# Second product of 24 leaves in seven half-width block products, with VectorE block sums

## The chip, the cores and the metric

The kernel runs on one core of one Trainium2 chip. The metric is the device time of one execution in microseconds (us). The engines have names in the profile: PE is the tensor engine (PEld its weight loads), DVE is VectorE, ACT is ScalarE, POOL is GpSimd, SP issues most transfers.

## The reference

`x` has 4 batches of 3072 tokens and 256 features. The reference takes the real part of a two-dimensional Fourier transform over tokens and features and then runs two feed-forward layers:

```
h = max(x @ w_in, 0);  u, v = h[..., :512], h[..., 512:]
v_n = (v - mean(v)) / sqrt(var(v) + 1e-6)
v_s = einsum('ts,bsd->btd', w_spatial, v_n) + b_spatial
x2 = (u * v_s) @ w_out                       # 512 features to 256
gate = 1 / (1 + exp(-(x2 @ w_gate)));  out = (gate * (x2 @ w_val)) @ w_out2
```

The change touches the product with `w_out`, called the second product here.

## The kernel before

**Number format.** Every matrix operand is split in a high and a low part (float32r). `mm3` (L259) makes three matmuls of one product: high x high, high x low, low x high (L261, L262, L263). The high part is a copy on ACT, the low part a subtraction on DVE.

**Stages.** First the transform and the product with `w_in` (to about 254 us). Then the product over tokens with `w_spatial` in "leaves" (to about 1751 us). Then the last feed-forward layer in 144 groups.

**Leaves.** The product over tokens is a seven-product scheme on 2x2 blocks: for each of two batch pairs `p`, seven products `i` in `ORDER` (L234), each in three column parts `c`: 42 leaves. A leaf has six steps `kp`, each of 24 matmuls of 512 columns into four PSUM banks `ps[d]`. The banks alternate between two sets of four. The stretch of the span in which PE works on one leaf is called a slot below; it lasts 32.64 us, or 38.08 us with a second product in it.

**Order of the work.** There is no scheduler: each engine runs its instructions in the order of the program text. At the beginning of each of the first four steps, `evacuate` (L1211) takes one bank `d` of the leaf before: DVE adds it to accumulators. For four of the seven products (`FINAL`, L236; 24 leaves) a token block of the gate is then complete: DVE multiplies by `u` (L1240), ACT copies the high part (L1246) and DVE forms the low part one step later (L1248). Then `advance` (L963) prepares operands `LEAD` = 3 steps ahead: loads on SP's queue, normalization on ACT (L916), sums or differences of blocks on DVE (L929, L933), high part on ACT (L942), low part on DVE (L950). In the last column part (`c` = 2) it also prepares the `v` operands of the next product. Loads go to seven tiles in rotation, and a load waits until the low part that last read its tile is done. `side_loads` (L1262) at the fifth step loads the bias and two `u` tiles, behind those loads on SP's queue. The matmuls of the step follow.

**The second product** of the leaf before runs after the fifth and after the sixth step of a slot (`second`, L1276): for each half `o` of the 256 outputs, four blocks `d` of 128 features, `mm3` each: 24 matmuls of 512 columns per leaf, into two banks that `evacuate` has emptied. ACT copies each bank to `x2` (L1287) and issues one store (L1289).

**The end of the stage.** The last slot (L1414 to 1467) orders its matmuls by bank, evacuates both the leaf before and its own banks 0 to 2, splits weights of the next stage and runs steps of the first operands there (`x_steps`, L1343). In the first feed-forward group (`n` = 0, L1552) come `p12` (two products, DVE adds them at L1484), the evacuation of bank 3, the split of "t1" (`steps[6]`), `p67`, both halves of the last second product (L1579, L1580) and `p5`, which uses "t1" (L1524).

Of the kernel before, what the change touches and what calls it, by code (L numbers as in the profile page):

```python
# [23 lines left out]
DM = 256  # L24
FF2 = 1536
P = 128
# [134 lines left out]
def layouts(x, moe_w_in, moe_w_spatial, moe_b_spatial, moe_w_out, moe2_w_gate, moe2_w_val, moe2_w_out):  # L161
# [18 lines left out]
    for at in (0, 32, 64):  # L180
# [6 lines left out]
    wg, wv = (w.reshape(2, P, 12, P) for w in (moe2_w_gate, moe2_w_val))  # L187
    arrays = {
# [6 lines left out]
        "w_out": moe_w_out.reshape(4, P, DM).transpose(1, 0, 2).reshape(P, 2, 512),  # L195
# [44 lines left out]
def tile_kernel(ctx: ExitStack, tc: tile.TileContext, t: dict, out: bass.AP):  # L240
# [927 lines left out]
    wo = [gp.tile([P, 2, 512], F32R, tag=f"wo{n}", name=f"wo{n}") for n in "hl"]  # L1168
# [3 lines left out]
    taken, begun, stores = [], [], []  # L1172

    def background():
# [5 lines left out]
        elif begun:  # L1180
            first, kind, i = begun.pop()
            value, = from64_rest(first, new())
            if kind == "second":
                split(wo[0][:, i, :], wo[1][:, i, :], value)
            elif kind == "out":
                stores.append((wv_d[i // 2][:, i % 2 * 512 : i % 2 * 512 + 512], value))
            else:
# [11 lines left out]
                stores.append((wg_d[i][:, 0:384], value[:, 0:384]))  # L1199
                stores.append((wg_d[i][:, 384:896], sums))  # L1200
        else:
            for to, value in stores:
                nc.sync.dma_start(to, value)
            stores.clear()
# [6 lines left out]
    def evacuate(leaf, ps, d, side):  # L1211
# [6 lines left out]
        if i in FINAL:  # L1218
            g = gp.tile([P, 512], F32, tag="cv", name="g", bufs=4)
# [21 lines left out]
        if "parts" in side:  # L1241
            gh, gl = (x[at] for x in side["parts"])
        else:
            gh = gp.tile([P, 512], F32R, tag="gh", name="gh", bufs=4)
            gl = gp.tile([P, 512], F32R, tag="gl", name="gl", bufs=4)
        nc.scalar.copy(gh, g)  # L1246
        finish_gate(side)
        side["low"] = lambda: nc.vector.tensor_tensor(out=gl, in0=g, in1=f(gh), op=ALU.subtract)  # L1248
        side["g"].append((gh, gl))
        if d < 2:  # L1250
            load_u(side, d + 2)

    def finish_gate(side):
        if "low" in side:
            side.pop("low")()
# [20 lines left out]
    def second(leaf, o, bank, side):  # L1276

        p, i, c = leaf
        mem, th = FINAL[i]
        finish_gate(side)  # L1280
        ps = banks(bank)
        for d in range(4):
            at = (d % 2) * 256 + o * P
            mm3(ps, [w[:, d // 2, at : at + P] for w in wo], side["g"][d], d == 0, d == 3)
        if o == 0:
            side["x2"] = gp.tile([P, 2, 512], F32, tag="x2", name="x2", bufs=1)
        nc.scalar.copy(side["x2"][:, o, :], ps)  # L1287
        if o == 1:
            nc.scalar.dma_start(x2_d[(2 * p + mem) * 6 + 3 * th + c], side["x2"])  # L1289
# [68 lines left out]
    def load_raw(j):  # L1358
        raw = []
        for c, n in zip(pairs[j], "hl"):  # L1360
            r = gp.tile([P, 2, 512], F32, tag=f"wo{n}", name="raw")
            nc.sync.dma_start(r, x2_d[c])
            raw += [r[:, 0, :], r[:, 1, :]]
        return raw
# [14 lines left out]
    for n, leaf in enumerate(leaves[:-1]):  # L1379
# [3 lines left out]
        side = {"g": []}  # L1383
        for kp in range(6):
            if before is not None:
                if kp < 4:
                    evacuate(before[0], before[1][kp], kp, before[2])
                else:
                    finish_gate(before[2])
# [15 lines left out]
            if before is not None:  # L1405
                if kp >= 4 and before[0][1] in FINAL:
                    second(before[0], kp - 4, 4 - base + kp - 2, before[2])
# [9 lines left out]
    side = {"g": []}  # L1417
# [19 lines left out]
    finish_gate(before[2])  # L1437
# [3 lines left out]
    side["parts"] = [cp.tile([P, 4, 512], F32R, tag=f"c0{k}", name=f"tail{k}") for k in range(2)]  # L1441
# [190 lines left out]
```

## Time and profile before

| | |
|---|---|
| median of 3 runs | 2842.18 us (2842.17 to 2842.79) |
| the profiled execution | 2841.18 us |
| its span, first to last instruction | 2839.1 us |
| PE busy | 2827.8 us, 12630 matmuls |
| DVE busy | 1998.9 us |
| ACT busy | 1416.4 us |
| granted PE clock | 1.0 (2.4 GHz) over the span |

The span leaves out about 2 us around the instructions. A matmul's row is longer than its distance to the next one, since matmuls are pipelined; the distances of starts tell the pace.

### The profile page before, as it was taken

Reading aid. Unit: us, or ns where it says so; the run is one execution under the profiler, and the core shown is the slowest. Engines: PE = TensorE matmul, PEld = TensorE weight load, DVE = VectorE, ACT = ScalarE, POOL = GpSimd, SP = SyncE. Lnnn points to the kernel's source line nnn. Section 1 sums busy time; section 2 is a strip of 40 time slices with the busy share of each in tenths; the row PEclk is TensorE's granted clock in tenths of the full one; section 3 lists DMA queues with packets and bytes.
Section 4 is the critical chain, followed back from the end, with each engine's and each line's share of the span. In section 5 each row is a group of like instructions: output and inputs, shape, how many; then the busy total and the mean of one; then the engine's idle time right before and its main releaser. Section 6 shows DMA issues by size and latency. Waiting matters only on the chain.

```text
span 2839.1 us, 34286 instructions
## 1 busy us (share of the span) xinstructions
PE 2827.8 (100%) x12630; PEld 2360.2 (83%) x12630; DVE 1998.9 (70%) x2936; ACT 1416.4 (50%) x2264; POOL 235.5 (8%) x348
## 2 busy tenths in 40 slices
PE   9999999999999999999999999999999999999999
PEld 7998888888888888888888888888888888888887
DVE  8877757778847666677756666876667666766665
ACT  6886434334424424433424424665655565656565
POOL 5984000011000000000000000000000000000000
PEclk9999999999999999999999999999999999999999
DMA  8888757778847766677866683100000000000000
GB/s 300 292 314 324 274 198 260 266 261 299 275 143 261 257 227 238 213 268 262 284 207 213 214 285 108 61 23 30 30 30 1 30 30 30 23 8 30 30 15 15
DMA packets 150953, 470.89 MB, mean 166 GB/s; under 512 B 16769, under 2 KB 18689, under 8 KB 150401
## 3 DMA queue, kind: packets, MB, share of 16 engines
q1 hardware_dynamic: 144448, 440.52, 45.0%
q0 software_dynamic: 2448, 14.82, 1.4%
q10 hardware_dynamic: 3888, 13.37, 1.2%
q8 instruction: 98, 1.61, 0.2%
q14 instruction: 71, 0.57, 0.1%
HBM read 386.07 MB, written 82.58 MB: 165 GB/s over the span
## 4 chain that ended last, share of the span: by engine, by line
PE 96%; DVE 2%; DMA 1%; ACT 1%; issue 0%; SPq 0%; ACTq 0%; DVEq 0%
PE bank L261 30%; PE bank L262 30%; PE bank L263 30%; PE psv L262 1%; PE psv L263 1%; PE psv L261 1%; PE psu L261 1%; PE psu L262 1%; PE psu L263 1%; PE psf L261 1%; PE psf L262 1%; PE psf L263 1%; DMA st<-v_d 1%; PE psv L730 0%; PE psu L768 0%
## 5 line engine op out<-in xcount | busy, mean ns | idle before, releaser
L262 PE MATMUL bank<-wl,vh 128*128 128x512 f32 x2016 | 784.4, 389 | 0.2 <-DVE wl L950 0.2
L261 PE MATMUL bank<-wh,vh 128*128 128x512 f32 x2016 | 784.3, 389 | 0.0
L263 PE MATMUL bank<-wh,vl 128*128 128x512 f32 x2016 | 784.2, 389 | 0.0
L942 ACT CAST wh<-st 128x1024 fp32r<-128x1024 f32 x249 | 260.9, 1049 | 382.9 <-PE bank L263 231.0
L262 PEld LDWEIGHTS bank<-wl,vh 128*128 128x128 f32 x2016 | 378.4, 188 | 79.5 <-DVE wl L950 0.8
L261 PEld LDWEIGHTS bank<-wh,vh 128*128 128x128 f32 x2016 | 378.4, 188 | 78.5
L263 PEld LDWEIGHTS bank<-wh,vl 128*128 128x128 f32 x2016 | 378.4, 188 | 78.3
L950 DVE TENSOR_TENSOR wl<-st,wh 128x1024 fp32r<-128x1024 f32 x249 | 306.8, 1233 | 169.4 <-ACT wh L942 168.9
L261 PE MATMUL bank<-x,wgh 128*128 128x512 f32 x673 | 262.4, 390 | 0.5 <-ACT t L1511 0.4
L1497 DVE TENSOR_TENSOR t<-t,bank 128x512 f32<-128x512 f32 x144 | 98.9, 687 | 231.4 <-PE bank L263 231.4
L262 PE MATMUL bank<-x,wgh 128*128 128x512 f32 x673 | 261.8, 389 | 0.0
L263 PE MATMUL bank<-x,wgl 128*128 128x512 f32 x673 | 261.8, 389 | 0.0
L933 DVE TENSOR_TENSOR st<-st 128x1024 f32<-128x1024 f32 x177 | 217.7, 1230 | 50.5 <-DMA st<-in_wt 50.5
L1520 DVE TENSOR_TENSOR gl<-s,gh 128x512 fp32r<-128x512 f32 x288 | 199.4, 692 | 57.8 <-ACT gh L1518 44.4
L262 PE MATMUL bank<-gl,wv 128*128 128x512 f32 x576 | 224.1, 389 | 0.0
L261 PE MATMUL bank<-gh,wv 128*128 128x512 f32 x576 | 224.1, 389 | 0.0
L263 PE MATMUL bank<-gh,wv 128*128 128x512 f32 x576 | 224.1, 389 | 0.0
L916 ACT ACTIVATE st<-st,ln_all 128x512 f32<-128x512 f32 x162 | 123.3, 809 | 140.5 <-DMA st<-v_d 115.7
L1485 ACT ACTIVATE s<-s 128x512 f32<-128x512 f32 x144 | 91.0, 632 | 153.8 <-DVE s L1484 153.7
L261 PEld LDWEIGHTS bank<-x,wgh 128*128 128x128 f32 x673 | 126.3, 188 | 28.5 <-ACT s L1482 0.9
L263 PEld LDWEIGHTS bank<-x,wgl 128*128 128x128 f32 x673 | 126.3, 188 | 26.3
L262 PEld LDWEIGHTS bank<-x,wgh 128*128 128x128 f32 x673 | 126.3, 188 | 26.0
(267 smaller groups left out, 4490.4 us busy)
## 6 DMA issues: line engine op xcount, KB each, us to landing
st<-in_wt SPq DMA_DIRECT2D x424, 512.0 KB, 5.5
st<-v_d SPq DMA_DIRECT2D x140, 512.0 KB, 4.7
u_d<-tu SPq DMA_DIRECT2D x64, 384.0 KB, 5.4
u<-u_d SPq DMA_DIRECT2D x96, 256.0 KB, 5.7
v_d<-tv SPq DMA_DIRECT2D x92, 256.0 KB, 5.1
x_d<-x ACTq DMA_DIRECT2D x24, 512.0 KB, 4.9
raw<-x_d SPq DMA_DIRECT2D x24, 512.0 KB, 7.1
xt<-in_xh SPq DMA_DIRECT2D x23, 512.0 KB, 5.2
```

The source lines that it names most:

```text
L261: nc.tensor.matmul(out=ps, lhsT=w[0], rhs=x[0], start=first, stop=False, **kw)
L262: nc.tensor.matmul(out=ps, lhsT=w[0], rhs=x[1], start=False, stop=False, **kw)
L263: nc.tensor.matmul(out=ps, lhsT=w[1], rhs=x[0], start=False, stop=last, **kw)
L916: nc.scalar.activation(st[:, k, :], st[:, k, :], AF.Identity, scale=scale[:, at], bias=shift[:, at])
L933: nc.vector.tensor_tensor(out=tiles[0], in0=tiles[0], in1=tiles[1], op=op)
L942: nc.scalar.copy(hl[0], st)
L950: eng.tensor_tensor(out=hl[1], in0=st, in1=f(hl[0]), op=ALU.subtract)
L1485: nc.scalar.activation(s1, s1, AF.Sigmoid)
L1497: nc.vector.tensor_tensor(out=g["t2"], in0=g["t2"], in1=g["b"], op=ALU.add)
L1520: nc.vector.tensor_tensor(out=l, in0=s, in1=f(h), op=ALU.subtract)
```

## The change

The second product is computed by the same kind of seven-product scheme. The 512 features of a leaf are two pairs of blocks of 128, the 512 tokens two halves of 256. Per pair there are seven terms, each `mm3` on 256 columns: 42 matmuls of 256 columns per leaf. The weights' sums and differences are formed once in the background work (POOL and DVE). Per pair DVE makes four differences of 128x256, and the operands of the terms are four pieces (one of 256 columns, three of 512), each with a high and a low part. Each piece has one buffer for both pairs. Four banks accumulate the seven terms over both pairs.

Six terms of the first pair run after the third step of a slot, the seventh after the fourth, all seven of the second pair after the fifth. `combine` then makes the outputs from the four banks: one copy on ACT and six additions on DVE; it stands in front of the sixth step's preparations. Two stores of half the size replace one. In the last leaf, six terms run before the feed-forward stage, the seventh in its first group and the second pair in its second group; the raw operands of the second pair of chunks are loaded one group later. All four banks of the other set are used instead of two.

```diff
@@ def background():
-            if kind == "second":
-                split(wo[0][:, i, :], wo[1][:, i, :], value)
...
+                for at, src in ((slice(0, 384), value[:, 0:384]), (slice(384, 896), sums)):
+                    if kind == "second":
+                        split(wo[0][:, i, at], wo[1][:, i, at], src)
@@ def evacuate(leaf, ps, d, side):
         nc.vector.scalar_tensor_tensor(out=g, in0=side["u"][d], scalar=0.0, in1=g, op0=ALU.max, op1=ALU.mult)
-        nc.scalar.copy(gh, g)
-        finish_gate(side)
-        side["low"] = lambda: nc.vector.tensor_tensor(out=gl, in0=g, in1=f(gh), op=ALU.subtract)
-        side["g"].append((gh, gl))
         if d < 2:
             load_u(side, d + 2)
+        finish_gate(side)
+        if d % 2 == 0:
+            side["raw"] = g
+            if d == 0:
+                take_piece(side, 0, 0, g[:, 0:HC])
+            return
+        b1, b2 = side.pop("raw"), g
+        if d == 1:
+            take_piece(side, 0, 1, b2)
+        else:
+            take_piece(side, 1, 0, b1[:, 0:HC])
+            side["late"] = lambda: take_piece(side, 1, 1, b2)
...
+        for to, x, y in (
+            (ta[:, 0:HC], b1[:, HC:], b1[:, 0:HC]),
+            (tb[:, 0:HC], b2[:, HC:], b1[:, HC:]),
+            (ta[:, HC:], b2[:, HC:], ta[:, 0:HC]),
+            (tb[:, HC:], b2[:, 0:HC], ta[:, HC:]),
+        ):
+            tt(out=to, in0=x, in1=y, op=ALU.subtract)
+        take_piece(side, d // 2, 2, ta)
+        take_piece(side, d // 2, 3, tb)
+    HC = 256
+    def take_piece(side, pair, i, src):
...
+        nc.scalar.copy(hi, src)
+        side["g"][pair, i] = (hi, lo)
+        side["lows"].append(lambda: nc.vector.tensor_tensor(out=lo, in0=src, in1=f(hi), op=ALU.subtract))
+    TERMS = {
+        1: ("a11", 0, 0, 0, 0), 6: ("s2", 2, 1, 0, 1), 5: ("s1", 2, 0, 1, 0), 7: ("s3", 3, 0, 1, 1),
+        3: ("s4", 1, 1, 2, 0), 4: ("a22", 3, 1, 2, 1), 2: ("a12", 1, 0, 3, 0),
+    }
+    def combine(side, part, both, to):
+        x, y, z, w = (side["acc"][k] for k in range(4))
+        nc.scalar.copy(p1, x[:, 0:HC])
+        tt(out=u2, in0=p1, in1=x[:, HC:], op=ALU.add)
+        tt(out=both, in0=u2 (twice), in1=y, op=ALU.add)
+        tt(out=to[1][:, HC:], in0=both[:, HC:], in1=y[:, 0:HC], op=ALU.add)
+        tt(out=to[0][:, HC:], in0=both[:, 0:HC], in1=z[:, 0:HC], op=ALU.add)
+        tt(out=to[1][:, 0:HC], in0=both[:, HC:], in1=z[:, HC:], op=ALU.add)
+        tt(out=to[0][:, 0:HC], in0=p1, in1=w[:, 0:HC], op=ALU.add)
@@ the loop over leaves
+            if final and kp == 4:
+                before[2].pop("late")()
+                finish_gate(before[2])
+            if final and kp == 5:
+                combine_cv(before[2])
             advance(6 * n + kp + LEAD, 2)
...
-            if before is not None:
-                if kp >= 4 and before[0][1] in FINAL:
-                    second(before[0], kp - 4, 4 - base + kp - 2, before[2])
+            if final and kp in (2, 3, 4):
+                second(before[2], kp // 4, ((1, 6, 5, 7, 4, 3), (2,), (1, 6, 5, 7, 4, 3, 2))[kp - 2], 4 - base)
+            if final and kp == 5:
+                send(before[0], before[2])
@@ the last slot
         if d == 0:
+            second(before[2], 0, (1, 6, 5, 7, 4, 3, 2), 4 - base)
+            before[2].pop("late")()
+            finish_gate(before[2])
...
         if d == 1:
-            second(before[0], 0, 4 - base + 2, before[2])
+            second(before[2], 1, (1, 6, 5, 7, 4, 3, 2), 4 - base)
+            combine_cv(before[2])
...
         if d == 2:
-            second(before[0], 1, 4 - base + 3, before[2])
+            send(before[0], before[2])
...
+    second(side, 0, (1, 6, 5, 7, 4, 3), base)
@@ the feed-forward groups
         if n == 0:
             evacuate(leaf, ps[3], 3, side)
+            second(side, 0, (2,), base)
+            side.pop("late")()
             finish_gate(side)
             steps[6]()
...
+            if n == 1:
+                second(side, 1, (1, 6, 5, 7, 4, 3, 2), base)
...
-            second(leaf, 0, base, side)
-            second(leaf, 1, base + 1, side)
+        if n == 1:
+            combine(side, x[:, 2, :], x[:, 3, :], [last_x2[:, o, :] for o in range(2)])
+            send(leaf, side)
...
-            if fb == 0:
+            if fb == (j == 0):
                 next_steps = x_steps(j + 1, load_raw(j + 1))
```

## Rows read from the trace of the kernel before

**Rows 1.** The page, part 1: busy time, share and instructions of each engine.

```profile
PE 2827.8 (100%) x12630; PEld 2360.2 (83%) x12630; DVE 1998.9 (70%) x2936; ACT 1416.4 (50%) x2264; POOL 235.5 (8%) x348
```

**Rows 2.** Timeline of PE, a leaf: start, length, line, shape; 36 rows between.

```profile
1299.77 0.39 PE L263 MATMUL bank<-wh,vl 128*128 128x512 f32 x1
...
1308.15 0.39 PE L261 MATMUL bank<-wh,vh 128*128 128x512 f32 x1
```

**Rows 3.** Timeline of weight loads and matmuls at a restart of PE.

```profile
1331.88 0.19 PEld L262 LDWEIGHTS bank<-wl,vh 128*128 128x128 f32 x1 [0.64 <-DVE wl L950]
1331.99 0.19 PEld L263 LDWEIGHTS bank<-wh,vl 128*128 128x128 f32 x1
...
1331.88 0.50 PE L262 MATMUL bank<-wl,vh 128*128 128x512 f32 x1 [0.22 <-DVE wl L950]
1332.21 0.40 PE L263 MATMUL bank<-wh,vl 128*128 128x512 f32 x1
```

**Rows 4.** Windows, one slot each: length, then busy time and instructions of each engine.

```profile
422.80:460.88 38.08, 38.08 (x170) 31.53 (x169) 31.63 (x38) 22.79 (x28) 0.00 (x0) 1.00 0.82 275
460.88:498.95 38.07, 38.07 (x169) 31.53 (x168) 27.45 (x33) 9.89 (x12) 0.00 (x0) 1.00 0.68 235
...
732.88:770.96 38.08, 38.08 (x170) 31.53 (x169) 32.13 (x39) 22.62 (x28) 0.00 (x0) 1.00 0.89 287
...
1712.64:1750.72 38.08, 38.08 (x169) 31.54 (x168) 25.17 (x34) 15.22 (x23) 0.00 (x0) 1.00 0.31 100
```

The columns after the length are PE, PEld, DVE, ACT, POOL, the granted PE clock, the DMA share and GB/s.

**Rows 5.** Timeline of PE in the transform, 384 columns; 8 rows between.

```profile
116.47 0.33 PE L261 MATMUL psf<-c,fh 128*128 128x384 f32 x1
...
118.03 0.33 PE L446 MATMUL psf<-spc,sps 128*128 128x384 f32 x1
```

**Rows 6.** Groups by line and shape: weight loads of the second product; busy, mean ns.

```profile
L261 PEld LDWEIGHTS bank<-gh,woh 128*128 128x128 f32 x184 | 34.5, 188 | 7.2
```

**Rows 7.** Timeline of DVE: 512 columns in the slot from 422.80, then 256 columns.

```profile
427.34 0.68 DVE L1224 TENSOR_TENSOR c<-bias,bank 128x512 f32<-128x512 f32 x1
427.94 0.68 DVE L1240 SCALAR_TENSOR_TENSOR g<-u,g 128x512 f32<-128x512 f32 x1
...
1760.97 0.42 DVE L257 TENSOR_TENSOR wgl<-wst,wgh 128x256 fp32r<-128x256 f32 x1
```

**Rows 8.** Timeline of DVE: third gate multiplications, and a fourth block's low part.

```profile
471.51 0.68 DVE L1240 SCALAR_TENSOR_TENSOR g<-u,g 128x512 f32<-128x512 f32 x1
...
747.30 0.68 DVE L1240 SCALAR_TENSOR_TENSOR g<-u,g 128x512 f32<-128x512 f32 x1
...
760.78 0.69 DVE L1248 TENSOR_TENSOR gl<-g,gh 128x512 fp32r<-128x512 f32 x1
```

**Rows 9.** Timeline of DVE from 422.80: its idle times, with what ended them.

```profile
425.60 1.23 DVE L950 TENSOR_TENSOR wl<-st,wh 128x1024 fp32r<-128x1024 f32 x1 [3.01 <-ACT wh L942]
...
456.99 1.46 DVE L929 SCALAR_TENSOR_TENSOR st<-st,ln_all 128x512 f32<-128x512 f32 x2 [2.36 <-ACT st L916]
...
461.86 0.69 DVE L1224 TENSOR_TENSOR c<-bias,bank 128x512 f32<-128x512 f32 x1 [1.40 <-DMA bias<-in_bt]
```

**Rows 10.** Timeline of ACT: the copy of the second product's bank.

```profile
423.00 0.59 ACT L1287 COPY x<-bank 128x512 f32<-128x512 f32 x1 [5.21 <-PE bank L263]
```

**Rows 11.** Timeline of DVE and PE in the first feed-forward group.

```profile
1752.36 0.68 DVE L1484 TENSOR_TENSOR s<-s,bank 128x512 f32<-128x512 f32 x1
...
1755.66 0.69 DVE L257 TENSOR_TENSOR x<-raw,x 128x512 fp32r<-128x512 f32 x1
...
1759.35 0.39 PE L261 MATMUL bank<-x,wgh 128*128 128x512 f32 x1
```

More of the change, by code (lines that the diff above doesn't have):

```diff
@@ L1172, in tile_kernel, with send_stores @@
     taken, begun, stores = [], [], []
+    def send_stores():
+        for to, value in stores:
+            nc.sync.dma_start(to, value)
+        stores.clear()
     def background():
@@ L1182, in background @@
             value, = from64_rest(first, new())
-            if kind == "second":
-                split(wo[0][:, i, :], wo[1][:, i, :], value)
-            elif kind == "out":
+            if kind == "out":
                 stores.append((wv_d[i // 2][:, i % 2 * 512 : i % 2 * 512 + 512], value))
@@ L1274, in side_loads, with second @@
                 load_u(side, d)
-    def second(leaf, o, bank, side):
+    TERMS = {
+        1: ("a11", 0, 0, 0, 0),
+        6: ("s2", 2, 1, 0, 1),
+        5: ("s1", 2, 0, 1, 0),
+        7: ("s3", 3, 0, 1, 1),
+        3: ("s4", 1, 1, 2, 0),
+        4: ("a22", 3, 1, 2, 1),
+        2: ("a12", 1, 0, 3, 0),
+    }
+    def second(side, pair, terms, bank):
+        for term in terms:
+            w, piece, half, acc, at = TERMS[term]
+            first = acc not in side["acc"]
+            if first:
+                side["acc"][acc] = banks(bank + acc)
+            w = slice(W_AT[w] * P, W_AT[w] * P + P)
+            mm3(
+                side["acc"][acc][:, at * HC : at * HC + HC],
+                [x[:, pair, w] for x in wo],
+                [x[:, half * HC : half * HC + HC] for x in side["g"][pair, piece]],
+                first,
+                pair == 1,
+                skip_group_check=True,
+            )
@@ L1278, in second, with combine_cv, send @@
+    def combine_cv(side):
+        combine(side, *(lambda a: (a[0], a[1], a[2:]))([gp.tile([P, 512], F32, tag="cv", name="y", bufs=4) for _ in range(4)]))
+    def send(leaf, side):
         p, i, c = leaf
         mem, th = FINAL[i]
[L1280 to L1286, printed above, removed]
@@ L1287, in second @@
-        nc.scalar.copy(side["x2"][:, o, :], ps)
-        if o == 1:
-            nc.scalar.dma_start(x2_d[(2 * p + mem) * 6 + 3 * th + c], side["x2"])
+        for o in range(2):
+            nc.scalar.dma_start(x2_d[(2 * p + mem) * 6 + 3 * th + c][:, o, :], side["to"][o])
     p, i, c = leaves[-1]
@@ L1436, in tile_kernel @@
         evacuate(before[0], before[1][d], d, before[2])
-    finish_gate(before[2])
     wv0 = [cp.tile([P, 8, DM], F32R, tag=f"c1{k}", name=f"wv{k}") for k in range(2)]
     wvs += [[x[:, 0:4, :] for x in wv0], [x[:, 4:8, :] for x in wv0]]
-    side["parts"] = [cp.tile([P, 4, 512], F32R, tag=f"c0{k}", name=f"tail{k}") for k in range(2)]
+    side["spare"] = cp.tile([P, 4, 512], F32, tag="c00", name="spare")
     steps = x_steps(0, [raw[:, k, :] for k in range(4)])
@@ L1558, in tile_kernel @@
         if n == 0:
+            side["parts"] = [cp.tile([P, 4, 512], F32R, tag=f"c0{k}", name=f"tail{k}") for k in range(2)]
             evacuate(leaf, ps[3], 3, side)
+            second(side, 0, (2,), base)
+            side.pop("late")()
             finish_gate(side)
```

76 lines of the change are left out of this document (48 added, 28 removed).

## The prediction

> **What bounds the kernel now.** I read the page's engine totals first: the tensor engine (PE) is busy for the whole span, VectorE for 70% and ScalarE for 50% [rows 1]. A busy PE can still be a PE that waits inside its rows, so the next view is the order of the matmuls: 37 steps between the two rows of 128x512 take 8.38 us, 0.2265 us each, and nothing but PE itself lies between them [rows 2]. In the two stages after the transform (leaves, then feed-forward) the stream is gapless, apart from a handful of waits of 0.1 to 0.6 us; the restart in [rows 3] is one of the largest. So time is saved only by a shorter stream, and lost by every new wait of PE. The last view is VectorE per slot (the stretch in which PE works on one leaf): it differs widely around its mean. In the slot from 422.80 it is busy for 31.63 of 38.08 us, in the next for 27.45, in the one from 732.88 for 32.13 [rows 4]. That is where a VectorE that gets more work can become the bound.
>
> **What the change does to PE.** Per leaf the second product goes from 24 matmuls of 512 columns to 42 of 256 (7 terms, 2 pairs, 3 parts each). The sizes in the trace are 512 columns at 0.2265 us [rows 2] and 384 at 1.56 us for 9 steps, 0.1733 us [rows 5]. The line through both falls by 0.0532 per 128 columns and gives 0.120 for 256. So 5.44 us become 42 x 0.120 = 5.04: 0.40 less per leaf, 9.6 for the 24 leaves. No row has this kind of matmul at 256 columns. Bounds: in proportion (0.113) it is 16.1 less; with no gain below 384 columns (0.173) it is 44 more. I take the line, because the thing that could break it, the load of weights ahead of each matmul, is shown at a restart to be fast enough: the second load starts 0.11 us after the first, and the restarting matmul starts its successor 0.33 us later, which is one load and one 0.2265 step [rows 3]. 0.11 fits under 0.120, barely.
>
> A weight-load row itself lasts 188 ns [rows 6], longer than 0.120. The Trainium skill (Perfetto Trace Analysis, "Identifying the Most-Contended Engine") says that matmul busy time is no measure of headroom and that the busy share of weight loads is; read so, a load holds the port for 188 ns, and 1008 of them take 189.5 us where the sum above has 121. The trace leans against that reading: at 384 columns matmuls with a load each follow at 173 ns, less than 188 [rows 5, 6].
>
> **What it adds on VectorE.** An operation on 512 columns holds VectorE 0.60 us (the distance of two starts), on 256 columns 0.34 (its row of 0.42, less the 0.08 by which rows overlap) [rows 7]. Per leaf: eight subtractions, 8 x 0.34 = 2.7; low parts of seven pieces and a half instead of four blocks, 2 x (0.34 + 3 x 0.60) = 4.3 against 2.4, so 1.9; the combination, 5 x 0.34 + 0.60 and some 0.1 for steps that wait on the one before, 2.4. Together 7.0. ScalarE gets the same larger pieces but one small copy for two large ones, about 1 us, and 0.33 for a second store on its queue; at 50% busy I cost that at nothing. If it were not hidden it would show as later high parts, in the waits below.
>
> **Where this meets PE.** The deadlines move. Before, all four blocks were wanted after the fifth of a slot's six steps; now the first pair is wanted after the third, 3 x 5.44 = 16.3 us after the slot starts, and its third piece 0.36 later, at 16.7. That piece's low part stands on VectorE's queue after the third gate multiplication (L1240): 0.60 for that, 1.36 for the subtractions before it, 0.34 more for two low parts where there was one of the block, and the low part itself at 0.68: about 3.0 us behind the place where that row starts now. In the slot from 460.88 the row starts at 471.51, 10.6 after the slot's start [rows 8]; that leaves 16.7 - 13.6 = 3.1 us for any delay D that VectorE brings along.
>
> D comes from the slot before, 422.80. There the combination stands in front of the last step's preparations. At the slot's start it costs nothing: VectorE idled 3.01 us there for a high part [rows 9], because ScalarE was held until 423.00 by the copy of the second product's bank [rows 10], and that copy now comes a step earlier. The 4.6 us of subtractions and low parts remain. The slot's own combination, 2.4, falls where VectorE waits 2.36 for a load [rows 9], and gives that load its time. Small dependent steps add 0.4: D = 5, a wait of 1.9 us. At the low end the 1.40 wait for the bias [rows 9] also soaks up work and D stays under 3.1: no wait. At the high end nothing is soaked up: D = 7, 3.9 us. Four slots are of this kind (first third of a weight group after a last third, with a two-block preparation): 4 x 1.9 = 7.6.
>
> In the slot from 732.88 VectorE prepares two blocks each of both operands, and the third multiplication starts at 747.30, 14.4 after its start [rows 8]: 17.4 with the 3.0, so 0.7 late even with D = 0 (the combination in front again takes the place of a ScalarE wait). The second pair is wanted at 29.7 + 0.36 + 0.7 = 30.8; the fourth block's low part starts now at 760.78, 27.9 in [rows 8], and 2.3 of the first pair's and 1.1 of its own work come before: 31.3, done at 32.0, another 1.2 late. With its twin in the second half: 2 x 1.9 = 3.8. Between 0 and 5 each. In all other slots the third multiplication comes early enough or VectorE has idle time for the 7.0.
>
> What is queued behind: the pieces have one buffer, so ScalarE's high parts of the second pair wait until PE has used the first (16.7). Normalizations and high parts of weights three steps ahead stand behind them, due 15 us later: covered. On SP's queue, loads wait for tiles that VectorE's low parts release, and bias and u loads stand behind those; they move with D and are in its upper end. The 24 stores, doubled and halved, are waited for only much later.
>
> **The end of the stage.** In the last slot VectorE is busy 25.17 of 38.08 [rows 4]; it gets 7.0 for one leaf and 2.3 for the last leaf's first pair. PE does that pair's six terms before the feed-forward begins, reaching it 1.8 us later than now. VectorE adds the first two products (L1484) at 1752.36, 1.6 after that point now [rows 11, 4]; I put it at 42.9 into the slot, 3.2 later than now, since part of its idle time there is waiting for PE that stays. The seventh term writes the bank that VectorE's next operation frees, 1.28 later at 44.2; PE is there at 41.2: 3.0 us of waiting. Then the matmuls of p5 (L1524) need a split that ends now at 1756.35, 4.0 after the addition began [rows 11]. Now six operations more stand between, 5.98 plus some 0.2: it is ready at 49.1, PE at 45.9. Before, 5.44 us of second product covered that (PE got there at 1759.35 [rows 11]); it has moved to other places. So 3.2 more; less 0.8 of PE gain for these two leaves and 0.4 of small waits there now: +5.0. Bounds: -0.8 (all hidden) and +9 (a similar wait once more in the next group).
>
> **Sum.** Twenty-two leaves in the loop, -8.8; their waits, 7.6 + 3.8 = +11.4 (0 to 25); the end, +5.0 (-0.8 to +9). That is +7.6 on the profiled execution's 2841.18, 2848.8; the median of the runs shown, 2842.18, lies 1.0 above it: 2849.8.
>
> **Rivals.** (1) The cover holds: loads land earlier once ScalarE is not held at the slot's start, D stays near 3 and the end hides half of its work. Then -9.6 + 2 for the two heavy slots + 2 at the end: 2836. For it: VectorE's idle time over a pair of slots, 38.08 + 38.07 less 31.63 and 27.45, is 17 us for 14 added [rows 4]. Against it: much of that idle is waiting on loads that are issued only when VectorE releases tiles. It decides where D is under 3.1. Chance 0.28, of which 0.17 lies beyond 0.2% faster (5.7 us, about what a measurement of this kernel can tell from no change). (2) The combination comes so late that the next leaf's first bank is not free: it has one step of 5.44 us, and a VectorE 3 us later than I have it misses that in some eight slots, with D then growing from slot to slot. 2860 to 2875. Chance 0.10. (3) Weight loads bind at 256 columns. At 0.173 each, 1008 x 0.053 = 53 more: 2903. At 188 ns by the rule above, 68 more: 2918. Against: the 0.11 between loads. Chance 0.07 together.
>
> **How the numbers follow.** The forecast case, PE's gain given back in VectorE waits, has 0.55 and its own range 2842 to 2859; 0.35 of it lies above 2847.9, 0.20 within 0.2%. Faster: 0.17. Same: 0.20 and 0.11 of the first rival, 0.31. Slower: 0.35 + 0.10 + 0.07 = 0.52. The range leaves out the weight loads, the top of the second rival and a little below 2836: 2836 to 2866.
>
> **What would show it.** Right: 42 matmuls of 256 columns per leaf at 0.12 us; PE waits "<- DVE" for a piece's low part in the four slots and two heavier ones, 1 to 4 us each, and none elsewhere; two waits of about 3 us in the first feed-forward group; VectorE about 168 us busier. Wrong: matmul distances at 256 columns away from 0.12; PE gapless in the leaf slots; waits of PE on a bank that the combination reads.

## The result and the profile after

| | before | changed |
|---|---|---|
| median | 2842.40 us (5 runs, 2842.17 to 2846.56) | 2869.52 us (5 runs, 2866.07 to 2876.0) |
| profiled execution's span | 2839.1 us | 2867.7 us |
| ahead of the first leaf's first matmul | 254.1 us | 254.7 us |
| the 42 leaves | 1496.4 us | 1514.2 us |
| from the last leaf's last matmul to the end | 1088.6 us | 1098.8 us |

The ratio is 1.0094, 95% interval 1.0077 to 1.0111: 27 us slower. The forecast was 7.6 us slower, and the range ended at 2866. So the direction was right and the size was not. Of the 28.5 us between the spans, 0.6 lie ahead of the leaves, 17.8 in them and 10.1 behind.

The pace of PE came as forecast. The page's totals (part 1), and the first and last of 17 matmuls in the second feed-forward group, on PE's timeline:

```profile
PE 2834.7 (99%) x13062; PEld 2382.2 (83%) x13062; DVE 2170.1 (76%) x3370; ACT 1443.3 (50%) x2338; POOL 240.2 (8%) x356
```

```profile
1786.68 0.28 PE L262 MATMUL bank<-tail,woh 128*128 128x256 f32 x1
...
1788.59 0.28 PE L263 MATMUL bank<-tail,woh 128*128 128x256 f32 x1
```

16 steps take 1.91 us, 0.119 each. VectorE is 171 us busier than in [rows 1] (168 forecast). The windows of nine stretches, eight slots and the first feed-forward group (length, then PE, PEld, DVE, ACT, POOL with instructions, granted PE clock, DMA share, GB/s):

```profile
423.96:461.70 37.74, 37.74 (x187) 32.06 (x186) 36.75 (x56) 21.60 (x29) 0.00 (x0) 1.00 0.74 257
461.70:504.64 42.94, 39.33 (x187) 33.43 (x186) 35.91 (x53) 13.05 (x18) 0.00 (x0) 0.96 0.68 222
700.56:739.52 38.96, 37.99 (x188) 32.11 (x186) 36.22 (x56) 14.22 (x20) 2.21 (x4) 1.00 0.81 259
739.52:777.98 38.46, 38.32 (x188) 32.16 (x186) 37.30 (x56) 22.69 (x31) 0.00 (x0) 1.00 0.87 282
891.20:930.24 39.04, 37.99 (x188) 32.10 (x186) 37.01 (x55) 14.62 (x20) 0.00 (x0) 1.00 0.81 276
1216.86:1260.78 43.92, 40.77 (x187) 34.48 (x186) 37.15 (x54) 14.35 (x19) 0.00 (x0) 0.92 0.73 253
1495.66:1541.23 45.57, 40.27 (x187) 34.13 (x186) 39.92 (x58) 24.14 (x32) 0.00 (x0) 0.93 0.85 283
1654.45:1693.64 39.19, 37.98 (x187) 32.10 (x186) 37.30 (x56) 14.77 (x20) 0.00 (x0) 1.00 0.81 278
1768.87:1786.00 17.13, 12.71 (x48) 9.76 (x47) 14.64 (x26) 9.11 (x17) 0.00 (x0) 0.70 0.05 9
```

An undisturbed slot lasts 37.74 us where it lasted 38.08 [rows 4]: 0.34 less, 7.8 in the 23 slots that have a second product. Against that stand the slots from 461.70, 1216.86 and 1495.66 (called A, B and C) with 5.2, 6.2 and 7.8 us over 37.74, the four others shown with 4.7 together, and two slots without a second product (from 352.63 and 1326.06) with 1.7 more than before. The last row is the beginning of the feed-forward.

Two things are to be seen. The waits of A, B and C are far longer than the 1.9 us forecast. And behind them the granted clock is under 1.0, which no step of the prediction had. PE's timeline in slot C:

```profile
1517.91 0.58 PE L263 MATMUL bank<-bl,woh 128*128 128x256 f32 x1 [5.30 <-DVE bl L1287]
1518.29 0.41 PE L264 MATMUL bank<-bh,wol 128*128 128x256 f32 x1
1518.51 0.41 PE L262 MATMUL bank<-bh,woh 128*128 128x256 f32 x1
...
1521.07 0.63 PE L262 MATMUL bank<-wh,vh 128*128 128x512 f32 x1
1521.49 0.63 PE L263 MATMUL bank<-wl,vh 128*128 128x512 f32 x1
```

After a wait of 5.3 us for a piece's low part the matmuls follow at 0.21 and 0.43 us instead of 0.12 and 0.23: 1.2 GHz instead of 2.4. What a slot is over 37.74, less PE's wait (from the one matmul's start to the next, less the normal step: 3.8, 3.3 and 5.5 us), is the clock's part: 1.4 us in A, 2.9 in B, 2.4 in C. In the first feed-forward group the 21 matmuls from 1776.37 to 1785.99 take 8.6 us without the wait between them, where at full clock they take 4.4; with 0.2 off for two restarts, 4.0 of that is the clock. Together 10.7 us, more than a third of the loss.

Why is PE's wait in A so long? Two loads on SP's queue before (in the slot ahead of the one from 460.88), then the same two in the changed kernel, then VectorE there:

```profile
452.38 2.60 SPq L882 DMA_DIRECT2D st<-in_wt  x2
455.04 0.42 SPq L1267 DMA_DIRECT2D bias<-in_bt  x1
```

```profile
457.65 5.56 SPq L883 DMA_DIRECT2D st<-in_wt  x2
463.26 0.42 SPq L1306 DMA_DIRECT2D bias<-in_bt  x1
```

```profile
460.13 0.41 DVE L1358 TENSOR_TENSOR y<-y,bank 128x256 f32<-128x256 f32 x1
460.46 1.22 DVE L934 TENSOR_TENSOR st<-st 128x1024 f32<-128x1024 f32 x1
461.59 1.22 DVE L951 TENSOR_TENSOR vl<-st,vh 128x1024 fp32r<-128x1024 f32 x1
...
469.60 0.69 DVE L1231 TENSOR_TENSOR c<-bias,bank 128x512 f32<-128x512 f32 x1 [3.73 <-DMA bias<-in_bt]
```

The bias load was issued 5.8 us ahead of its slot and is now issued 1.6 us behind its start. It stands behind the second operand load, which goes out when VectorE's low part at 461.59 is done, and that low part stands behind the combination (its last row is the one at 460.13). VectorE then waits 3.73 us where it waited 1.40 [rows 9]. In C the wait for the bias is 4.93 us. In B it is only 0.18: there VectorE waits 1.75 us for a normalization, which waits for its operand load.

### The profile page after: what moved, and what is told of

Same layout as the page of the kernel before. It is cut to its first block, busy times and chain, and to the rows that moved or that the text cites. A ratio compares the mean times of both kernels' runs of the same rounds, so it can differ in the third digit from the quotient of the medians.

```text
span 2867.7 us, 35792 instructions
## 1 busy us (share of the span) xinstructions
PE 2834.7 (99%) x13062; PEld 2382.2 (83%) x13062; DVE 2170.1 (76%) x3370; ACT 1443.3 (50%) x2338; POOL 240.2 (8%) x356
## 4 chain that ended last, share of the span: by engine, by line
PE 74%; DVE 11%; DMA 7%; issue 4%; ACT 2%; SPq 0%; POOL 0%; DVEq 0%; ACTq 0%; POOLq 0%
PE bank L263 22%; PE bank L262 22%; PE bank L264 22%; DMA st<-v_d 3%; DVE wl L951 2%; DVE st L934 2%; DMA words<-in_w_b 1%; DVE vl L951 1%; DVE bl L1287 1%; PE psv L263 1%; ACT st L917 1%; PE psv L264 1%; PE psv L262 1%; DVE st L930 1%; PE psu L262 1%
## 5 line engine op out<-in xcount | busy, mean ns | idle before, releaser
L951 DVE TENSOR_TENSOR wl<-st,wh 128x1024 fp32r<-128x1024 f32 x249 | 307.2, 1234 | 46.7 <-ACT wh L943 46.5
```

What stands on the lines that cost most here:

```text
L951: eng.tensor_tensor(out=hl[1], in0=st, in1=f(hl[0]), op=ALU.subtract)
```

## The experiments

**The bias load's place.** `side_early` moves the bias and u loads ahead of the fifth step's operand loads:

```diff
+            if kp == 4:
+                side_loads(leaf, side)
             advance(6 * n + kp + LEAD, 2)
-            if kp == 4:
-                side_loads(leaf, side)
```

> The bias and u loads are issued ahead of the fifth step's operand loads instead of behind them; nothing else changes. Theory A (the three large waits, in the slots that start at 461.70, 1216.86 and 1495.66 in the changed kernel, come from the bias load, which stands on SP's queue behind an operand load that waits for a tile that VectorE releases only after its combination): VectorE's waits of 3.73 and 4.93 us for the bias go, the slots of 42.94, 43.92 and 45.57 us fall to about 39 each as in the slots that need no bias, the granted clock stays at 1.0 in them, and the run falls by about 15 us, to 2851 to 2857. Theory B (VectorE simply has too much work, and the wait for the bias only takes the place of a wait that would come later): the three slots stay within 1.5 us each, and the run within 5 us of 2869. Possible side effect: the operand loads behind are 1.3 us later, which would show as new waits on st.

Measured: 2854.62 us, ratio 1.0045 (1.0030 to 1.0060), 15 us less. The windows of slots A, B and C in this run:

```profile
461.99:499.87 37.88, 37.88 (x187) 32.10 (x186) 35.90 (x53) 13.60 (x19) 0.00 (x0) 1.00 0.75 257
1210.84:1253.09 42.25, 39.56 (x187) 33.34 (x186) 36.53 (x54) 14.35 (x19) 0.00 (x0) 0.96 0.75 260
1487.90:1527.54 39.64, 38.49 (x187) 32.16 (x186) 37.53 (x56) 23.91 (x32) 0.00 (x0) 1.00 0.87 291
```

VectorE no longer waits for a bias anywhere. A and C come down as theory A has it; B only by 1.7. There the operand loads are the later ones: VectorE waits 2.18 us for a normalization, the third gate is late again, and PE waits 2.9 us, with a lower clock after it. So the place of the bias and u loads was the larger part (the leaves take 1498.9 us, 15.3 less), and not the whole.

**VectorE's amount of work.** `no_subs` leaves out the four differences per pair; pieces 2 and 3 are the token blocks themselves:

```diff
-            tt(out=to, in0=x, in1=y, op=ALU.subtract)
-        take_piece(side, d // 2, 2, ta)
-        take_piece(side, d // 2, 3, tb)
+        take_piece(side, d // 2, 2, b1)
+        take_piece(side, d // 2, 3, b2)
```

> Leaves out the four differences per pair on VectorE (2.7 us per leaf); the pieces 2 and 3 are split from the two token blocks themselves. Theory A: the slots in which VectorE only has too much work (starts 700.56, 891.20, 1654.45; waits 1.1, 1.2 and 1.3 us) lose their waits; the three large waits shrink by about 2 us each for the 1.4 us that come earlier in the own slot and what is carried over, but the wait for the bias stays over 1.5 us, since the combination still stands ahead of the tile's release; the run falls by 10 to 14 us, with the clock's part. Theory B (VectorE's sum of work decides): all leaf waits go, the run falls by over 22 us.

Measured: 2849.77 us, ratio 1.0028 (1.0016 to 1.0040), 20 us less, between the two expectations. All leaf waits over 0.2 us go but two: slot C keeps 5.2 us on a piece (45.43 us long), with a wait of VectorE for the bias of 5.55, and the slot of 33.94 in the changed kernel still lasts 33.53. In A the wait for the bias stays too, as theory A has it; VectorE in this run:

```profile
466.76 0.69 DVE L1231 TENSOR_TENSOR c<-bias,bank 128x512 f32<-128x512 f32 x1 [3.54 <-DMA bias<-in_bt]
```

But it ends 5.5 us after the slot's start, where it ended 7.9 after it, and with that and the slot's own differences gone PE does not wait in A or B at all, which theory A did not expect. This fits one loop: VectorE late, tile late, load late, bias late, and VectorE late again in the next slot.

**The clock.** `filler` puts additional matmuls (their results are overwritten) ahead of the one that waits in A, B and C:

```diff
+            if fill and k == 1:
+                side["acc"][2] = banks(bank + 2)
+                for _ in range(fill):
+                    mm3(side["acc"][2][:, 0:HC], ...
```

> In the same three slots PE gets 24, 21 and 36 additional matmuls of 256 columns (2.9, 2.5 and 4.3 us) right ahead of the matmul that waits for VectorE; their results are overwritten, and they are shorter than the waits of 3.65, 3.2 and 5.35 us that they stand in. Theory C (after a long wait PE is granted 1.2 GHz for some us, and that alone costs 1.4, 2.9 and 2.4 us in these slots): with the waits cut to about 1 us the granted clock stays at 1.0 there, the slots become 1.4 to 2.9 us shorter though PE does more work, and the run falls by 5 to 7 us. Rival (the clock falls for another reason, the wait is not its cause): the clock still falls to 0.5 after the same places, and the run stays within 2 us or gets longer.

Measured: 2869.43 us, ratio 1.0094 (1.0077 to 1.0111), no change. In A and B the clock is 1.00 and the slots last 42.62 and 40.41; in C the filling matmuls themselves wait 3.72 us for their bank (the third bank is evacuated just ahead of the piece), the clock falls to 0.93, and the slot lasts 48.66. With that flaw the total says nothing of theory C. `filler2` is the same with the second bank (`banks(bank + 1)`), which is free by then:

> As the run filler, but the additional matmuls (24, 21 and 36, that is 2.9, 2.5 and 4.3 us) write a bank that is already free, so that they fill the wait from its beginning in all three slots (starts 461.70, 1216.86, 1495.66 in the changed kernel; waits 3.65, 3.2 and 5.35 us). Theory C (a long wait is followed by 1.2 GHz): granted clock 1.0 in all three slots, the slots 41.4, 41.0 and 43.1 us (37.74 plus the wait) instead of 42.94, 43.93 and 45.57, the run 5 to 7 us shorter than the changed kernel although PE computes 9.7 us more. Rival (the clock falls whatever PE does there): clock 0.92 to 0.96 as before, slots not shorter.

Measured: 2864.01 us, ratio 1.0074 (1.0057 to 1.0091), 5.5 us less with 81 matmuls more. Windows of A, B and C:

```profile
462.00:503.34 41.34, 40.87 (x212) 34.98 (x210) 35.88 (x53) 12.92 (x18) 0.00 (x0) 1.00 0.70 237
1215.90:1256.16 40.26, 40.26 (x208) 34.58 (x207) 36.48 (x54) 14.45 (x19) 0.00 (x0) 1.00 0.76 259
1495.71:1539.85 44.14, 42.80 (x224) 36.46 (x222) 38.34 (x57) 24.15 (x32) 0.00 (x0) 1.00 0.81 274
```

The clock stays at 1.00 in all three, and they are 1.6, 3.7 and 1.4 us shorter although PE computes more in them. Theory C holds: the clock fell because PE had waited. The slots show this, and not the total: the runs of the two kernels overlap (2862.6 to 2867.7 here, 2866.1 to 2876.0 there), and in the profiled one two other slots are 6.3 us longer than in the changed kernel (from 888.64 and 1321.44). The second of these has a wait of 2.9 us for an operand; there the clock falls to 0.91.

**The combination's place.** `combine_late` moves it behind the last step's preparations:

```diff
-            if final and kp == 5:
-                combine_cv(before[2])
             advance(6 * n + kp + LEAD, 2)
+            if final and kp == 5:
+                combine_cv(before[2])
```

> Only the combination is moved, behind the last step's preparations. Theory A (the combination ahead of the preparations holds the tile for which the operand load ahead of the bias waits): the bias lands 2 to 3 us earlier, the three large waits shrink by 2 to 3 us each and fall under the length that costs clock, the run falls by 8 to 12 us. Price: the combination ends about 2.4 to 4.6 us later, so in the slots in which VectorE is late at the end (those ahead of the starts 461.70, 891.20, 1216.86, 1654.45, and the one from 739.52) the next leaf's first matmul waits for the bank that it reads: 0 to 3 us each. Rival (only VectorE's sum of work counts): the three slots and the run stay within 3 us of the changed kernel, or the run gets longer by the new waits.

Measured: 2884.52 us, ratio 1.0147 (1.0132 to 1.0162). PE's waits in this run (in all, times, longest):

```profile
PE bank L262 <- DVE y L1348: 20.3, 6, 6.9
...
PE bank L263 <- DVE bl L1287: 4.1, 2, 2.4
```

VectorE's waits for the bias in A and C, 3.73 and 4.93 us in the changed kernel, are gone, so the combination did hold the loads. The waits for pieces fall from 15.3 us in six places to 4.1 in two; part of that is not the loads' doing, since PE itself reaches these slots later. But six times the next leaf's first matmul waits for the bank, up to 6.9 us, where 0 to 3 were put down. The run is 15 us longer than the changed kernel: ahead of the preparations is the better place.

**Differences on GpSimd.** `side_pool` is `side_early` with the block differences moved:

```diff
-            tt(out=to, in0=x, in1=y, op=ALU.subtract)
+            eng = nc.vector if "spare" in side and d == 3 else nc.gpsimd
+            eng.tensor_tensor(out=to, in0=x, in1=y, op=ALU.subtract)
```

> Bias and u loads ahead of the operand loads as in side_early, and the block differences on GpSimd instead of VectorE (about 0.77 us each there by the row of L381 at this size, 3.1 us per pair, 2.7 us per leaf less on VectorE). Theory: the two causes of the leaf waits are separate and add up: no slot of the leaves is over 38.5 us, the stretch of the leaves is 1496.4 less 7.5 plus 1 to 2, about 1490; the end stays about 1097; the run is 2840 to 2844. Rival (GpSimd's differences come too late for the high parts, or slow VectorE down): waits of PE for a piece's low part come back in many slots and the run stays over 2850.

Measured: 2885.51 us, ratio 1.0153 (1.0137 to 1.0168), 31 us more than `side_early`: the rival. Groups by line of GpSimd and of VectorE in this run (busy, mean ns, idle before):

```profile
L1274 POOL TENSOR_TENSOR t<-g 128x256 f32<-128x256 f32 x92 | 112.7, 1225 | 899.0 <-DVE g L1247 554.0 <-DMA x_d<-y 251.3 <-DVE bl L1288 90.8
```

```profile
L951 DVE TENSOR_TENSOR wl<-st,wh 128x1024 fp32r<-128x1024 f32 x249 | 328.5, 1320 | 54.7 <-ACT wh L943 54.5
```

A difference takes 1.22 us on GpSimd, not the 0.77 of its rows at this size in the transform, and VectorE's largest operation goes from a mean of 1234 ns in the changed kernel to 1320. PE waits 25 us for pieces.

**The deadline.** `late_terms` is `side_early` with the whole first pair behind the fourth step:

```diff
-            if final and kp in (2, 3, 4):
-                second(before[2], kp // 4, ((1, 6, 5, 7, 4, 3), (2,), (1, 6, 5, 7, 4, 3, 2))[kp - 2], 4 - base)
+            if final and kp in (3, 4):
+                second(before[2], kp - 3, (1, 6, 5, 7, 4, 3, 2), 4 - base)
```

> side_early, and all seven terms of the first pair after the fourth step of a slot instead of six after the third: the deadline of its pieces moves from 16.3 to 21.8 us after the slot's start; the second pair stays after the fifth. Theory E (what is left of the leaf waits in side_early, 0.7, 1.35, 4.5, 1.9 and 0.9 us in the slots from 739.5, 891.2, 1216.9, 1495.7 and 1654.5, is the early deadline of the first pair): these waits go but for the one from 739.5, the leaves take 1489 to 1492 us, the run 2845 to 2848. Rival (the pieces have one buffer: the second pair's high parts stand in ScalarE's queue until PE has read the first pair, 24.3 us after the slot's start, and its low parts are ready at 28 at best; the second pair at 29.7 becomes the late one, and normalizations behind them are late too): new waits on bl after the fifth step or on wl and vl at the next steps, 1 to 3 us in each slot that follows a heavy one, and no gain.

Measured: 2847.44 us, ratio 1.0018 (1.0009 to 1.0028), 7 us less than `side_early`. The leaves take 1494.7 us (1498.9 there). B lasts 38.41, the slots of 39.04 and 39.19 in the changed kernel 37.97 and 37.89; C lasts 40.67, 1.0 more than in `side_early`; 1.6 us of its waits are for a bank that VectorE still has to evacuate. Theory E holds but for C. Of the rival only a little shows: PE waits for weights' low parts (wl) three times, 2.1 us in all, instead of once for 0.9.

**The end of the stage.** `tail` puts the split of t1 ahead of the last evacuation and the seventh term in the second group:

```diff
-            evacuate(leaf, ps[3], 3, side)
-            second(side, 0, (2,), base)
+            steps[6]()
+            evacuate(leaf, ps[3], 3, side)
...
-            steps[6]()
...
+                second(side, 0, (2,), base)
                 second(side, 1, (1, 6, 5, 7, 4, 3, 2), base)
```

> Only the end of the stage: the split of t1 stands ahead of the last bank's evacuation, and the seventh term of the first pair runs in the second feed-forward group, ahead of the second pair. Theory: PE's wait of 3.56 us for the bank (1772.42) goes and with it the halved clock until 1786; in its place a wait of 1 to 2 us for t1's low part, and 0 to 2 us in the second group; the stretch from the end of the leaves to the end of the run gets 6 to 8 us shorter, the run 2861 to 2864. Rival (the stretch is bound by the amount of VectorE work between the first two groups, whatever its order): the waits move to the second group, and less than 3 us are gained.

Measured: 2867.33 us, ratio 1.0089 (1.0074 to 1.0104); the stretch behind the leaves is 1100.05 us, 1.3 longer. The long wait moved, to `p5`, which writes the bank that a copy of `p67` (L1599) has to read first. ScalarE in this run:

```profile
1775.60 1.66 ACT L1285 CAST tail<-c 128x512 fp32r<-128x512 f32 x3 [2.78 <-DVE c L1273]
1777.17 0.57 ACT L1599 COPY t<-bank 128x512 f32<-128x512 f32 x1
```

PE waited 4.79 us for the copy at 1777.17, which stood on ScalarE's queue behind the pieces' high parts, and these behind VectorE's differences. `tail_pool` is `tail` with the low parts of three weight splits of the last slot on GpSimd:

```diff
-            split_wv(0, staged_b[1])
+            split_wv(0, staged_b[1], nc.gpsimd)
...
-            split_wg(1, staged_b[2])
-            split_wv(1, staged_b[3])
+            split_wg(1, staged_b[2], nc.gpsimd)
+            split_wv(1, staged_b[3], nc.gpsimd)
```

> The end of the stage as in the run tail, and the low parts of three weight splits of the last slot on GpSimd (about 3.4 us less on VectorE there). Theory D (the end is bound by the amount of VectorE work between the last slot and the second group): the waits of 1.8, 1.0 and 5.4 us of the run tail shrink by 3 to 4 us together, the granted clock of the first groups stays at 1.0, the stretch after the leaves is 1091 to 1095 instead of 1098.8 and 1100.1. Rival (the chain of dependences in the first two groups sets it, not the amount): under 2 us less than in the run tail.

Measured: 2872.48 us, ratio 1.0103 (1.0088 to 1.0118), the stretch 1101.3 us: the rival. But this does not tell amount from order, since VectorE got nothing for it: where GpSimd works beside it, it takes longer. GpSimd, then VectorE beside it:

```profile
1757.53 2.84 POOL L258 TENSOR_TENSOR wv<-stb,wv 128x1024 fp32r<-128x1024 f32 x1
```

```profile
1757.30 3.61 DVE L258 TENSOR_TENSOR x<-raw,x 128x512 fp32r<-128x512 f32 x2
1760.84 0.67 DVE L1244 TENSOR_TENSOR c<-c,bank 128x512 f32<-128x512 f32 x1
```

Two low parts of 512 columns take 3.61 us there and 1.29 in the changed kernel. The second of them ends 0.54 us after GpSimd's operation, about its own length: it ran only then. `tail2` is `tail` with the pieces behind the bank copies, and one weight split later:

```diff
+        elif "spare" in side:
+            side["late"] = lambda: [
+                take_piece(side, 1, k, x) for k, x in enumerate((b1[:, 0:HC], b2, ta, tb))
+            ]
...
         if n == 0:
+            split_wv(1, staged_b[3])
             steps[7]()
+            side.pop("late")()
+            finish_gate(side)
```

> Only the end of the stage, and on other grounds than tail: there PE's long wait (5.4 us) ended with a copy of a bank on ScalarE that stood behind copies of the last pieces, which waited for VectorE's differences. So here the copies of the last pair's pieces stand behind those bank copies, the seventh term of the first pair is in the second group, the split of t1 ahead of the last evacuation, and one weight split (wv, 1.1 us) behind. Theory F (ScalarE's queue order made the wait of the second kind; VectorE's backlog only the first): the wait for the copy goes, a wait of about 1 to 2 us for VectorE's first addition stays, the granted clock stays at 1.0, the stretch after the leaves is 1090 to 1093 us instead of 1098.8; the run about 2861 to 2864. Rival (the amount of VectorE work): the wait goes over to the second group, where the pieces are wanted, and the stretch is over 1096.

Measured: 2868.34 us, ratio 1.0091 (1.0077 to 1.0105), the stretch 1100.65 us. Theory F held for the copy (no wait for it over 0.7 us), and the stretch got no shorter. VectorE in this run, and the matmul that waited for it:

```profile
1777.62 1.22 DVE L258 TENSOR_TENSOR wv<-stb,wv 128x1024 fp32r<-128x1024 f32 x1
...
1780.13 2.22 DVE L1293 TENSOR_TENSOR tail<-c,tail 128x256 fp32r<-128x256 f32 x4
1782.27 0.68 DVE L1618 TENSOR_TENSOR t<-t,bank 128x512 f32<-128x512 f32 x1
```

```profile
1783.01 0.79 PE L262 MATMUL bank<-x,wgh 128*128 128x512 f32 x1 [5.95 <-DVE t L1618]
```

The addition of `p5`, which frees a bank, now stood behind the low parts of pieces that are wanted later. `best2` joins `late_terms` and `tail2`:

> late_terms and tail2 together. If both theories hold: leaves 1489 to 1492, end 1090 to 1093, the run 2834 to 2841, so at or under the kernel before. If only the end's holds: 2843 to 2848.

Measured: 2850.57 us, ratio 1.0029 (1.0019 to 1.0040): leaves 1493.2, the stretch 1101.1; above both expectations, in the main because the end's theory was wrong. `best3` is `late_terms` with VectorE's and ScalarE's queues in the first two groups in the order of what PE wants next (the last differences and pieces, too, come behind `p5`):

```diff
+        if n == 1:
+            x = C[2][0]
+            combine(side, x[:, 2, :], x[:, 3, :], [last_x2[:, o, :] for o in range(2)])
         p67(n, prev)
...
+            split_wv(1, staged_b[3])
...
         if now:
             p5(n)
+        if n == 0:
+            steps[7]()
+            side.pop("late")()
+            finish_gate(side)
```

> late_terms with another end of the stage: in the first feed-forward group the addition of p5 and the split of t1 come ahead of the last differences and pieces on VectorE, ScalarE's bank copies ahead of the pieces' high parts, the seventh term is in the second group; there the combination stands ahead of the low parts of the gates. Theory G (the end is bound by the order on VectorE's queue: in tail2 the long wait, 5.9 us, was for p5's addition, which stood behind 5.4 us of differences and low parts that are wanted later): no wait of PE over 2 us, granted clock 1.0, the waits together 3 to 5 us; the stretch after the leaves is 1090 to 1093 us, the run 2838 to 2843, level with the kernel before. Rival (VectorE's amount of work between the last slot and the second group is what PE waits for in any order): waits and halved clock again, now for the pieces in the second group, the stretch 1096 or more, the run 2846 or more.

Measured: 2844.71 us, ratio 1.0007 (0.9998 to 1.0016), not to be told from the kernel before; the leaves take 1493.9 us and the stretch behind them 1094.1. PE's two longest sums of waits behind the transform, and the beginning of the feed-forward in a window:

```profile
PE bank L263 <- DVE wl L951: 2.6, 2, 1.8
PE bank L262 <- ACT t L1614: 1.5, 2, 0.8
```

```profile
1748.82:1766.00 17.18, 14.31 (x75) 10.90 (x74) 15.02 (x26) 10.43 (x18) 0.00 (x0) 1.00 0.01 2
```

The clock is 1.00 where it was 0.70. With the same VectorE work in another order 4.7 us of the 10.1 are back (7.0 against `best2`, which has the same leaves), and the long waits with the halved clock are gone: they came from the order, as theory G has it. The stretch is a microsecond over what was expected, and the run 1.7; what is left there are waits of about 1 us each, and whether another order takes these away was not tried. So in no order tried is the change a gain: the 8 us that PE saves went, in the best one, into waits that are left in the leaves and behind them.

## Why the prediction was right or wrong

- **PE's gain.** Right: 0.120 us forecast per matmul, 0.119 measured; 9.6 us forecast, about 8 measured (0.34 a slot instead of 0.40). (The bound in proportion is 16.3 less, not 16.1.) The third rival is out: matmuls with a load each follow faster than the 188 ns of a load's row. So the rule of the Trainium skill weighed in the prediction (Perfetto Trace Analysis, "Identifying the Most-Contended Engine") does not mean that load rows add up: at 85% busy loads in an undisturbed slot (32.06 of 37.74 us) PE shows no wait for one.
- **VectorE's added work.** Right: 7.0 us per leaf, 168 in all; 171 measured.
- **Which slots wait, and for what.** Mostly right: a piece's low part is late in all six slots named, and in one that was not (from 700.56, 1.1 us).
- **The sizes of these waits.** Too small, in C above all. In A the prediction's own terms hold (a low part 3.0 us behind the row's old place, and D). The second gate multiplication, which has none of the slot's new work ahead of it, starts 6.0 us after the start of A before and 12.7 after it now:

```profile
466.84 0.68 DVE L1240 SCALAR_TENSOR_TENSOR g<-u,g 128x512 f32<-128x512 f32 x1
```

```profile
474.45 0.69 DVE L1247 SCALAR_TENSOR_TENSOR g<-u,g 128x512 f32<-128x512 f32 x1
```

So D is 6.8 us in A, near the forecast's upper end of 7, and PE waits 3.8 where 3.9 was put down for that end. In the four slots of this kind (A, B, and those from 891.20 and 1654.45) D is 6.8, 5.3, 4.6 and 5.6 where 5 was put down, and the waits are 9.7 us together instead of 7.6. The wait for the bias did not soak up work; in A it grew from 1.40 to 3.73. (The low end, "D stays under 3.1", did not follow even from the prediction's numbers: 5 less 1.4 is 3.6.) C is one of the two heavy slots, and there the step "0.7 late even with D = 0 (the combination in front again takes the place of a ScalarE wait)" failed. Its third gate multiplication, before and in the changed kernel:

```profile
1499.04 0.68 DVE L1240 SCALAR_TENSOR_TENSOR g<-u,g 128x512 f32<-128x512 f32 x1
```

```profile
1515.97 0.68 DVE L1247 SCALAR_TENSOR_TENSOR g<-u,g 128x512 f32<-128x512 f32 x1
```

It starts 20.3 us after the slot's start instead of 14.9. Of these 5.4 us, 1.2 are the slot's own new work (in A, too, the third follows the second by 5.9 us instead of 4.7); the rest, 4.2, is a D that was put at 0, and PE waits 5.5 us where 1.9 was forecast and 5 was the bound. A delay of VectorE does not stop at VectorE. It delays the release of a tile, the load that waits for that tile and whatever stands behind it on SP's queue, and so comes back one slot later. `side_early`, which touches nothing but these loads' places, takes 15.3 us off the leaves. Without the clock's part the waits in the leaves are 18.9 us where 11.4 was forecast, still inside its bounds of 0 to 25.

- **The combination.** The step that laid it in a wait of VectorE for a load counted its 2.4 us and not that it waits itself: in the slot ahead of C VectorE idles 3.02 us in front of it until PE has done the second pair, with that step's preparations behind it. Before that it idles 3.51 us for a high part that waits for PE to have read its one buffer, which the prediction had down as covered. The bias load of C then goes out 1.2 us ahead of the slot's start, where it went out 13.4 ahead. Moving the combination costs more (`combine_late`).
- **The granted clock.** This is the step that failed first of all: the sum adds PE's waits by their length and puts what follows them at nothing, without a reason. The clock costs 6.7 us in A, B and C and 4.0 behind the leaves, 10.7 of the 20.9 by which the two spans differ more than forecast (28.5 against 7.6). The rest is 7.5 of longer waits in the leaves, 1.4 of PE's gain, 0.7 of waits at the end and 0.6 ahead of the leaves. Without these 10.7 the run would take about 2859 us (an estimate: 2869.5 less 10.7, if nothing else moved), inside the range. The term is missing even where the wait was forecast nearly right: the one for the bank at the end (3.0 forecast, 3.6 measured) had 4.0 of the clock behind it. In `filler2`, which does nothing but keep PE at work in the waits of A, B and C, the clock stays at 1.00 there and these slots are 6.7 us shorter together.
- **The end.** +5.0 forecast, +10.1 measured behind the last leaf (9.8 with the last slot, which the forecast's figure takes in). The wait for the bank was forecast at 3.0 and is 3.56. The one for t1 (3.2 forecast) did not come: that low part was done at 1781.25, and PE, at half its clock and after a wait of 0.86 us for a copy, came to the matmul that reads it only at 1781.38; the 4.0 of the clock, and small waits in the second group, make the rest.
- **Range and chances.** A loop of waits and a clock that falls after long ones are both reasons for a longer upper side than the range had; the rival of 2860 to 2875 had the right time with another mechanism, a bank freed late, of which the changed kernel shows nothing.

## What to carry to other kernels

When a step is added to an engine that releases load tiles, follow the delay along the load queue to the last transfer behind it, and give small loads with a near deadline a place ahead of loads that wait for tiles. Price a long wait of TensorE with what it costs afterwards at half the clock (here 1.4 to 4.0 us behind each wait of 3.3 us and more), not with its length alone. Order each queue by what TensorE wants next before you look for another engine to do the work.

## What was not expected of the hardware

- After the waits of 3.3 us and more in the changed kernel the granted clock was 1.2 GHz for some microseconds (0.21 us for 256 columns, 0.43 for 512); after those of 1.1 to 1.4 us it was not. In the other runs it went either way after waits of 2.7 to 2.9 us: in B it fell in `side_early` (2.9 us, 0.96 over the slot) and in `tail` (2.8, 0.96), but not in `tail_pool` (2.7, 1.00), and not in the slot from 888.64 of `filler2` (2.8, 1.00). So length alone does not tell it there; what does stays open.
- GpSimd and VectorE do not work side by side on these operations: 1.22 us instead of 0.77 for a difference on GpSimd, and 3.61 instead of 1.29 us for two low parts on VectorE beside one of 2.84 on GpSimd. The Trainium skill has the rule (SBUF — State Buffer, "Who interferes with whom"): a VectorE instruction with two inputs in SBUF contends with a GpSimd instruction that reads SBUF, for a port pair that only one of them can hold at a time. The rows of `tail_pool` agree: the second low part ends 0.54 us behind GpSimd's operation.
